# Two pools of tiles change places under the gated stage, and the Gelu's table is loaded at the head of the last block

## The chip, the cores and the metric

One core of one Trainium2 chip runs the whole program. The metric is device time of one execution in microseconds (us). The kernel before was executed three times, and one further execution was profiled.

## What is computed

A decaying linear attention (per token, a state of 64 x 64 per head, here written in chunks), then three bilinear products, then a gated layer. Cut to what matters:

```python
x = attention(q, k, v)                    # 4 x 768 tokens, 8 heads x 64
a, b = x @ w1, x @ w2                     # 512 -> 1024
x = (a * b @ w3) @ w_out                  # 1024 -> 512
h = x @ w_in                              # 512 -> 2048
g = h * (1.0 / (1.0 + np.exp(-1.702 * h)))
return g @ w_out2                         # 2048 -> 512
```

There are 3072 tokens. The weights arrive as 64-bit floats and are rebuilt on the chip.

## The kernel before

Every product of matrices is done three times, on a high part and a low part of each operand (`mm3`, L220 to L223), so that float32 accuracy comes out of a narrower multiplier. High parts are made by a cast, low parts by a subtraction.

The program has four stages, and in each the order of instructions on every engine is the order in which the code issues them (a manual schedule).

- **Attention** (L695 to L761), in 24 chunks, while ScalarE (ACT) and VectorE (DVE) rebuild weights and `w3 @ w_out` is formed.
- **The six blocks** of 512 tokens (L768 to L866). In each, `gate` (L798) makes two products of 12 matmuls and multiplies them, eight times, and `mixed` (L807) adds each into four accumulators. At a block's end the four accumulators are copied out by ACT (L825) and DVE (L823) in turn, into two tiles named `st` under the tag "st" and two under the tag "tmp", and SyncE (SP) stores each to `yd` in DRAM (L826, 256 KB each). The tokens of even blocks lie in one pair of tiles, those of odd blocks in another (`homes["x", 1]`, the pool `p1x`). The last block, number 5, is odd.
- **The gated stage** (`Expand`, L448), four passes over 768 tokens. One pass is eight `quad`s; each makes seven products P1, P5, P6, P2, P3, P7, P4 of six matmuls with 384 columns, and P4 of a quad is issued in the next one (`fourth`), after that one's P5. So the first quad of the stage has 36 matmuls and every later one 42. ACT copies P1, P5, P6 and P7 out of their banks (`copy`, L459) and applies the Gelu (`gated`, L469); DVE adds. A later product of the same bank starts only once ACT has copied the earlier one. Results go to tiles `g`, five buffers, two to a quad, and SP stores them to `gd` (L472, 384 KB each).
- **The last product** (`contract`, L617), from `gd` and `w_out2`.

The weights of the gated stage were split earlier and stored as sixteen blocks `sp` in DRAM. Eight of them, one to a quad, are brought back by eight DMAs of 1792 KB on GpSimd's (POOL's) queue: `run` calls `fetch_left` (L441) for quad n = 0 to 7, which fills the tile `op` of slot SLOT[n]. Those eight slots, and behind them the tiles `g` and the tiles `s` and `u` of `copy`, are laid over memory that the six blocks had used, and the framework puts in the waits that this needs. Per partition a slot takes 14336 bytes, so eight take 114688. Below them lie, from the bottom, the pool `big` (65536 bytes, weights), `p1w` (32768, weights), `p1x` (16384, the odd blocks' tokens) and `p1` (16384: "tmp", then the gate's results "h", then "st"). The first three make 114688 bytes too. So the slots end where `p1` begins, and `g` and `s` lie on `p1`:

```python
SLOT = 0, 1, 5, 6, 7, 2, 3, 4
...
homes = [left_tile(self.pf, x) for x in range(NQ)]
for n in range(NQ):
    fetch_left(n, homes[SLOT[n]])
```

The same table gives the slots that the last product reuses (`OPENING`, L599, and L678); they go by SLOT[n] throughout.

ACT has two loads of its activation table: at L107 at the start (Abs), and at L469, ahead of the first Gelu.

Of the kernel before, what the change touches and what calls it, by code (L numbers as in the profile page):

```python
# [7 lines left out]
F32 = mybir.dt.float32  # L8
F32R = mybir.dt.float32r
I32 = mybir.dt.int32  # L10
AF = mybir.ActivationFunctionType
# [5 lines left out]
P = 128  # L17
# [4 lines left out]
TB = 512  # L22
# [19 lines left out]
def tile_kernel(  # L42
# [13 lines left out]
    nc = tc.nc  # L56
# [1 line left out]
    big = first.enter_context(tc.tile_pool(name="big", bufs=1, reuse_waits="tile"))  # L58
    second, third = (ctx.enter_context(ExitStack()) for _ in range(2))
    edge = ctx.enter_context(tc.tile_pool(name="edge", bufs=1, side="right"))  # L60
    edge.tile([P, 88], F32, name="edge")
    prep = second.enter_context(
        tc.tile_pool(name="prep", bufs=1, side="right", reuse_waits="tile")
    )
# [150 lines left out]
    def weight(i):  # L215
        while complete <= i:
            work(1)
        return parts[i]
# [21 lines left out]
    def halves(key):  # L240
        return [tuple(t[:, d] for t in xhl[key]) for d in range(KD)]
# [191 lines left out]
    left = {}  # L433
    PART = dict(P1=0, P2=1, P4=2, P5=3, P6=4, P7=5, P3=6)

    SLOT = 0, 1, 5, 6, 7, 2, 3, 4

    def left_tile(pool, slot):
        return pool.tile([P, 2, 7, 256], F32R, tag=f"op{slot}", name="op")

    def fetch_left(n, t):  # L441
        left[n] = t
        nc.gpsimd.dma_start(t.rearrange("p a b c -> p a (b c)").bitcast(F32), sp[n])
# [4 lines left out]
    class Expand:  # L448
# [62 lines left out]
        def run(self):  # L511
            self.late, self.open = [], None
# [3 lines that stand above are left out]
            nxt = None  # L516
# [25 lines left out]
    def load_g(n, pool, queue=nc.sync, **at):  # L542
        if n >= len(batches):
            return
        i, b = batches[n]
        raw = raws2[n] = pool.tile([P, 2, 2, TB], F32, name="gr", **at)
        at = 0
        while at < TB:
            s, t0 = divmod(i * TB + at, 2 * TS)
            m = min(TB - at, 2 * TS - t0)  # L550
            for k in range(2):
                queue.dma_start(
                    raw[:, k, :, at : at + m], gd[s][:, 2 * b + k, :, t0 : t0 + m]
                )
            at += m

    def sums(n, pool, **at):
        (b11, b12), (b21, b22) = (
            [raws2[n][:, :, f, h * TU : (h + 1) * TU] for h in range(2)] for f in range(2)
        )  # L560
        t = mid[n] = pool.tile([P, 4, 2, TU], F32, name="gt", **at)
        for x, (a, b) in enumerate(((b12, b11), (b22, t[:, 0]), (b22, b12), (b21, t[:, 1]))):
            nc.vector.tensor_tensor(t[:, x], a, b, ALU.subtract)

    def operand_tiles(n, pool, tags, **at):
        ops[n] = [
            pool.tile([P, 7, 2, TU], F32R, tag=tag, name=f"o{w}", **at)
            for w, tag in zip("hl", tags)
        ]
# [18 lines left out]
    def split_piece(a, b):  # L588
# [3 lines left out]
        else:  # L592
# [7 lines left out]
        (0, 3): lambda p, pf: load_g(0, p, tag="raw"),  # L600
        (1, 3): lambda p, pf: sums(0, pf, tag=f"op{SLOT[0]}"),
        (3, 0): lambda p, pf: (
            operand_tiles(0, pf, [f"op{SLOT[x]}" for x in (1, 2)]),
            split_piece(0, 1),
        ),
        (3, 3): lambda p, pf: split_piece(1, 2),
        (4, 0): lambda p, pf: split_piece(2, 3),
        (4, 1): lambda p, pf: fetch_left(NQ, left_tile(pf, SLOT[3])),
        (4, 3): lambda p, pf: split_piece(3, 5),
        (5, 0): lambda p, pf: split_piece(5, 7),  # L610
        (5, 3): lambda p, pf: load_g(1, pf, tag=f"op{SLOT[0]}"),
        (5, 1): lambda p, pf: fetch_left(NQ + 1, left_tile(pf, SLOT[4])),
        (6, 1): lambda p, pf: fetch_left(NQ + 2, left_tile(pf, SLOT[5])),
# [76 lines left out]
    with tc.manual_schedule():  # L690
        with (
# [62 lines left out]
            while halves_done < 2 * KF:  # L754
                f = halves_done // 2
# [5 lines left out]
            mix_out()  # L761
        with (
            tc.tile_pool(name="p1w", bufs=1, reuse_waits="tile") as p1w,
            tc.tile_pool(name="p1x", bufs=1, reuse_waits="tile") as p1x,
            tc.tile_pool(name="p1", bufs=1, reuse_waits="tile") as p1,
            tc.tile_pool(name="ps1", bufs=1, space=PSUM, reuse_waits="tile") as ps1,
        ):
            homes["wd"], homes["x", 1] = p1w, p1x  # L768

            def reload(key, src, d):  # L770
                x = p1.tile([P, TB], F32, tag="st", bufs=2, name="xr")
                nc.sync.dma_start(x, src[:, d])
                return lambda: split(key, x, d)

            def mm(lhs, xs):
                ps = ps1.tile([P, TB], F32, tag="mm", bufs=4, name="psm")
                for d in range(KD):
                    mm3(ps, lhs[0][:, d], lhs[1][:, d], *xs[d], d == 0, d == KD - 1)
                return ps

            def pair(t):
                hi, lo = (
                    p1.tile([P, TB], F32R, tag="h", bufs=4, name=f"h{x}") for x in "hl"
                )
                nc.scalar.copy(hi, t)  # L785
                nc.vector.tensor_tensor(lo, t, hi.bitcast(F32), ALU.subtract)
                return hi, lo

            def tmp():
                return p1.tile([P, TB], F32, tag="tmp", bufs=2, name="tmp")  # L790


            xs = halves(order[0])
            ahead = None
            todo = []
            acc = None

            def gate(f, xs):  # L798
                w = [x.rearrange("p (m k f) -> p m k f", m=2, k=KD) for x in weight(W12 + f)]
                pa = mm([x[:, 0] for x in w], xs)  # L800
                pb = mm([x[:, 1] for x in w], xs)
                t = tmp()
                nc.scalar.copy(t, pa)
                nc.vector.tensor_tensor(t, t, pb, ALU.mult)  # L804
                return pair(t)

            def mixed(i, f, hl):  # L807
                nonlocal acc
                if f == 0:
                    acc = [  # L810
                        ps1.tile([P, TB], F32, tag=f"acc{e}", name=f"acc{e}")
                        for e in range(KD)
                    ]
                wh, wl = (x[:, f % 2 * DM : (f % 2 + 1) * DM] for x in wmix[f // 2])
                for e in range(KD):
                    r = slice(e * P, (e + 1) * P)
                    mm3(acc[e], wh[:, r], wl[:, r], *hl, f == 0, f == KF - 1)
                if f == KF - 1:
                    for e in range(KD):
                        tag = "st" if e < 2 else "tmp"  # L820
                        t = p1.tile([P, TB], F32, tag=tag, bufs=2, name="st")
                        if e % 2:
                            nc.vector.tensor_copy(t, acc[e])  # L823
                        else:
                            nc.scalar.copy(t, acc[e])  # L825
                        nc.sync.dma_start(yd[i][:, e], t)  # L826

            early = None
            for n, i in enumerate(order):
                last = n == NB - 1  # L830
                nxt = None if last else order[n + 1]
                for f in range(KF):
                    if not last and KF - KD - 2 <= f < KF - 1:
                        ready, ahead = ahead, None
                        if f < KF - 2:
                            ahead = reload(nxt, xd[nxt], f - KF + KD + 2)
                    if n == 0:
                        work_to(min(PAIR_OPS * (W12 + f + 2) + 4, PAIR_OPS * WI + 4))
                    elif not last:
                        work(5)  # L840
                    elif f == 0:
                        while complete < len(tiles):
                            work(1)
                        second.close()
                        py = third.enter_context(
                            tc.tile_pool(name="y", bufs=1, side="right", reuse_waits="tile")
                        )
                        early = operands(0, py)
                        next(early)
                    else:  # L850
                        next(early)
                    hl = gate(f, xs)
                    if todo:
                        late, *args = todo.pop()
                        late(*args)
                    todo.append((mixed, i, f, hl))
                    if not last and KF - KD - 1 <= f < KF - 1:
                        ready()
                    if 0 < n and not last:
                        work(4)  # L860
                    if last and f in (3, 6):
                        next(early)
                if nxt is not None:
                    xs = halves(nxt)
            late, *args = todo.pop()
            late(*args)  # L866
# [97 lines left out]
```

## Time and profile before

| | |
|---|---|
| three executions | 1052.08, 1053.18, 1053.92 us (median 1053.18) |
| the profiled execution | 1055.27 us, of which 1053.5 us is its span |
| PE (TensorE matmuls) busy | 1005.4 us, 95% of the span |
| DVE busy | 666.7 us, 63% |
| ACT busy | 405.5 us, 38% |
| POOL busy | 24.7 us, 2% |
| mean granted TensorE clock | 0.987 of full |

The page gives busy time by engine and the chain that ended last; the trace gives single instructions with their start, their duration and, in brackets, how long the engine had been idle and what ended that. "PEclk" is the granted clock: 1.00 is 2.4 GHz, 0.50 is 1.2 GHz. A DMA has two times, that of its issue (on SP's or POOL's queue) and its landing. q0 is the queue that POOL feeds, q1 that of SP.

### The profile page before, as it was taken

To read this page: it belongs to the slowest core of one execution; us is meant where nothing else is said; L and a number is where in the kernel's file an instruction comes from. 1 tells how busy PE (TensorE), PEld (TensorE's weight loads), DVE (VectorE), ACT (ScalarE), POOL (GpSimd) and SP (SyncE) were. 2 spreads that over 40 slices of the span, in tenths; PEclk is the share of its full clock that TensorE was granted. 3 is DMA by queue.
4 is the path that set the end of the run, shared out by engine and by line. 5 is a ranking of instruction groups with operands and counts; after the bars stand their busy time and mean duration, and the time that the engine had idled before them with its cause. 6 is when DMAs were issued, how large, how long until landed. Compare 5 with 4: busy or idle time off the path is not lost.

```text
span 1053.5 us, 16352 instructions
## 1 busy us (share of the span) xinstructions
PE 1005.4 (95%) x6528; PEld 914.8 (87%) x6528; DVE 666.7 (63%) x1084; ACT 405.5 (38%) x702; POOL 24.7 (2%) x49
## 2 busy tenths in 40 slices
PE   5789999999999999999994999999999999999997
PEld 4678787888888888888884999999999999999997
DVE  4998788856777767733440263453654597787783
ACT  2333334433434444321111555545555344334331
POOL 1110000000000000000000000000001000000000
PEclk9999999999999999999997899999999999999999
DMA  9998765436675766541319423424359943343431
GB/s 348 347 371 282 246 198 185 147 128 219 230 252 207 255 213 224 199 150 40 139 34 426 161 110 135 151 106 165 145 184 407 378 160 121 122 159 120 123 119 40
DMA packets 78012, 204.06 MB, mean 194 GB/s; under 512 B 6512, under 2 KB 28144, under 8 KB 72944
## 3 DMA queue, kind: packets, MB, share of 16 engines
q1 hardware_dynamic: 71744, 147.44, 40.3%
q0 software_dynamic: 6192, 55.58, 13.6%
q8 instruction: 51, 0.84, 0.3%
q14 instruction: 25, 0.20, 0.1%
HBM read 130.64 MB, written 72.35 MB: 193 GB/s over the span
## 4 chain that ended last, share of the span: by engine, by line
PE 84%; DMA 8%; DVE 4%; issue 3%; ACT 1%; POOL 0%; DVEq 0%; POOLq 0%; ACTq 0%
PE psm L223 8%; PE psm L221 8%; PE psm L222 8%; PE m L223 6%; PE m L222 6%; PE m L221 6%; PE acc L221 4%; PE acc L223 4%; PE acc L222 4%; PE a L221 4%; PE a L223 4%; PE a L222 4%; DMA gr<-gd 3%; DMA yd<-st 2%; PE e L221 2%
## 5 line engine op out<-in xcount | busy, mean ns | idle before, releaser
L221 PE MATMUL m<-oh,op 128*128 128x256 f32 x672 | 187.8, 279 | 0.5 <-DVE o L649 0.5
L223 PE MATMUL m<-oh,op 128*128 128x256 f32 x672 | 188.1, 280 | 0.0
L222 PE MATMUL m<-ol,op 128*128 128x256 f32 x672 | 187.7, 279 | 0.0
L223 PE MATMUL psm<-xh,wl 128*128 128x512 f32 x384 | 149.5, 389 | 1.5 <-DVE wl L116 1.5
L222 PE MATMUL psm<-xl,wh 128*128 128x512 f32 x384 | 149.4, 389 | 0.0
L221 PE MATMUL psm<-xh,wh 128*128 128x512 f32 x384 | 149.4, 389 | 0.0
L221 PEld LDWEIGHTS m<-oh,op 128*128 128x128 f32 x672 | 125.9, 187 | 0.8 <-DVE o L649 0.8
L222 PEld LDWEIGHTS m<-ol,op 128*128 128x128 f32 x672 | 126.3, 188 | 0.2 <-DVE ol L586 0.2
L223 PEld LDWEIGHTS m<-oh,op 128*128 128x128 f32 x672 | 126.3, 188 | 0.0
L221 PE MATMUL a<-yh,op 128*128 128x384 f32 x256 | 87.1, 340 | 15.3 <-ACT s L459 11.4
L804 DVE TENSOR_TENSOR tmp<-tmp,psm 128x512 f32<-128x512 f32 x48 | 33.0, 688 | 104.2 <-PE psm L223 93.3
L223 PEld LDWEIGHTS psm<-xh,wl 128*128 128x128 f32 x384 | 72.1, 188 | 17.0 <-DVE wl L116 2.0
L223 PE MATMUL a<-yh,op 128*128 128x384 f32 x256 | 86.7, 339 | 0.0
L222 PE MATMUL a<-yl,op 128*128 128x384 f32 x256 | 86.7, 338 | 0.0
L222 PEld LDWEIGHTS psm<-xl,wh 128*128 128x128 f32 x384 | 72.1, 188 | 15.0
L221 PEld LDWEIGHTS psm<-xh,wh 128*128 128x128 f32 x384 | 72.1, 188 | 14.9
L497 DVE TENSOR_TENSOR s<-c,s 128x384 f32<-128x384 f32 x32 | 17.8, 558 | 98.7 <-PE c L223 98.7
L584 ACT CAST oh<-gr 128x512 fp32r<-128x512 f32 x69 | 38.3, 618 | 102.7 <-PE m L223 59.9
L785 ACT CAST hh<-tmp 128x512 fp32r<-128x512 f32 x48 | 29.8, 621 | 121.7 <-DVE tmp L804 121.7
L221 PE MATMUL acc<-hh,wh 128*128 128x512 f32 x192 | 74.7, 389 | 0.0
L222 PE MATMUL acc<-hl,wh 128*128 128x512 f32 x192 | 74.7, 389 | 0.0
L223 PE MATMUL acc<-hh,wl 128*128 128x512 f32 x192 | 74.7, 389 | 0.0
(99 smaller groups left out, 1889.8 us busy)
## 6 DMA issues: line engine op xcount, KB each, us to landing
op<-sp POOLq DMA_DIRECT2D x16, 1792.0 KB, 11.4
gd<-g SPq DMA_DIRECT2D x64, 384.0 KB, 2.3
qkv<-in_qkv_dram POOLq DMA_DIRECT2D x23, 1024.0 KB, 8.1
raw<-in_w_dram SPq DMA_DIRECT2D x32, 512.0 KB, 5.2
gr<-gd SPq DMA_DIRECT2D x30, 512.0 KB, 4.8
raw<-in_wo_dram SPq DMA_DIRECT2D x24, 512.0 KB, 5.5
raw<-in_wi_dram SPq DMA_DIRECT2D x16, 512.0 KB, 5.0
sp<-wqh SPq DMA_DIRECT2D x16, 512.0 KB, 3.7
```

Source lines behind the costliest of these rows:

```text
L221: nc.tensor.matmul(ps, wh, xh, start=start, stop=False, skip_group_check=True)
L222: nc.tensor.matmul(ps, wh, xl, start=False, stop=False, skip_group_check=True)
L223: nc.tensor.matmul(ps, wl, xh, start=False, stop=stop, skip_group_check=True)
L497: nc.vector.tensor_tensor(s1, c, s1, ALU.add)
L584: nc.scalar.copy(h, x)
L785: nc.scalar.copy(hi, t)
L804: nc.vector.tensor_tensor(t, t, pb, ALU.mult)
```

## The change

Four edits. The pool `p1` is cut in two: `p1h` holds the tiles "h", and `p1` keeps "tmp" and "st". The pools are opened in the order `p1w`, `p1h`, `p1`, `p1x`, so that "h", "tmp" and "st" lie below 114688 bytes, under slot 7, and the odd blocks' tokens lie above, under `g` and `s`. SLOT is changed so that slot 7 is filled last, for quad 7, and slots 2, 3 and 4 for quads 4, 5 and 6. And a tile that was only a spacer is cleared by POOL at the start, and one element of it goes through the Gelu at the head of the last block.

```diff
-    edge.tile([P, 88], F32, name="edge")
+    still = edge.tile([P, 88], F32, name="edge")
+    nc.gpsimd.memset(still, 0.0)
...
-    SLOT = 0, 1, 5, 6, 7, 2, 3, 4
+    SLOT = 0, 1, 5, 6, 2, 3, 4, 7
...
             tc.tile_pool(name="p1w", bufs=1, reuse_waits="tile") as p1w,
+            tc.tile_pool(name="p1h", bufs=1, reuse_waits="tile") as p1h,
+            tc.tile_pool(name="p1", bufs=1, reuse_waits="tile") as p1,
             tc.tile_pool(name="p1x", bufs=1, reuse_waits="tile") as p1x,
-            tc.tile_pool(name="p1", bufs=1, reuse_waits="tile") as p1,
...
-                    p1.tile([P, TB], F32R, tag="h", bufs=4, name=f"h{x}") for x in "hl"
+                    p1h.tile([P, TB], F32R, tag="h", bufs=4, name=f"h{x}") for x in "hl"
...
                         next(early)
+                        nc.scalar.activation(still[:, :1], still[:, :1], AF.Gelu_apprx_sigmoid)
                     else:
```

Three lines are added above most of the program, so its line numbers grow by one to three in the kernel after. The order of the matmuls is the same, and that of DVE and SP too; what differs are ACT and POOL, and what instructions wait for.

**ACT, from the last block's end into the first quad.** Before (DMAHW is an SP transfer that must have landed, DMASW one of POOL's; s and u are the tiles of `copy`):

```order
L825 COPY st<-acc_4400 128x512 [waits PE_49,Activation_49]
L459 COPY s_4779<-a 128x384 [waits DMAHW3_49,DMAHW7_49,DVE_49,PE_49]
L459 COPY s_4787<-e 128x384 [waits PE_49]
L459 COPY u_4795<-a 128x384 [waits PE_49]
L469 ACT_TABLE_LOAD [waits DMAHW1_49,DMAHW0_49]
L469 ACTIVATE g<-s_4779 128x384 [waits DVE_49]
L459 COPY u_4818<-a 128x384 [waits PE_49]
L469 ACTIVATE g<-u_4795 128x384 [waits DVE_49]
L459 COPY s_4834<-a 128x384 [waits PE_49]
L469 ACTIVATE g<-u_4818 128x384 [waits DMAHW6_49,DVE_49]
```

Now:

```order
L827 COPY st<-acc_4405 128x512 [waits PE_49,Activation_49]
L460 COPY s_4785<-a 128x384 [waits PE_49]
L460 COPY s_4793<-e 128x384 [waits PE_49]
L460 COPY u_4801<-a 128x384 [waits PE_49]
L470 ACTIVATE g<-s_4785 128x384 [waits DVE_49]
L460 COPY u_4824<-a 128x384 [waits PE_49]
L470 ACTIVATE g<-u_4801 128x384 [waits DVE_49]
L460 COPY s_4840<-a 128x384 [waits PE_49]
L470 ACTIVATE g<-u_4824 128x384 [waits DVE_49]
```

The waits on the last block's stores (DMAHW7, 1, 0 and 6 are the second, fourth, third and first of its four) are gone, and with them the table load. It stands at the head of the last block, between the cast for the block before and the copy of the block's first gate:

```order
L787 CAST hh<-tmp 128x512 [waits DVE_49]
L852 ACT_TABLE_LOAD
L852 ACTIVATE edge<-edge 128x1
L805 COPY tmp<-psm 128x512 [waits PE_49,Activation_49]
L787 CAST hh<-tmp 128x512 [waits DVE_49]
```

**POOL, the weights of quads 2 to 7** (sp_85 to sp_90 before). Before:

```order
L443 DMA op<-sp_85 128x3584 [waits DMAHW2_49,DMAHW3_49,DMASW5_49,DMAHW5_49,DMASW0_49,DMAHW6_49,DVE_49,PE_49]
L443 DMA op<-sp_86 128x3584 [waits DMAHW2_49,DMAHW1_49,DMAHW3_49,DMASW7_49,DMAHW4_49,DMASW6_49,DVE_49]
L443 DMA op<-sp_87 128x3584 [waits DMAHW6_49,DMAHW7_49,DMAHW5_49,DMAHW0_49]
L443 DMA op<-sp_88 128x3584 [waits DMAHW4_49,DMAHW3_49,DMAHW5_49,DMAHW2_49,PE_49]
L443 DMA op<-sp_89 128x3584 [waits DMAHW4_49,DMAHW5_49,DMAHW3_49,DMAHW2_49]
L443 DMA op<-sp_90 128x3584 [waits DMAHW3_49,DMAHW2_49,DMAHW4_49,DMAHW1_49,Pool_49]
```

Now (sp_86 to sp_91):

```order
L444 DMA op<-sp_86 128x3584 [waits DMAHW2_49,DMAHW3_49,DMASW5_49,DMAHW5_49,DMASW0_49,DMAHW6_49,DVE_49,PE_49]
L444 DMA op<-sp_87 128x3584 [waits DMAHW1_49,DMAHW2_49,DMASW7_49,DMAHW3_49,DMASW6_49,DMAHW4_49,DVE_49,PE_49]
L444 DMA op<-sp_88 128x3584 [waits DMAHW6_49,DMAHW5_49,DMAHW7_49,DMAHW0_49,PE_49]
L444 DMA op<-sp_89 128x3584 [waits DMAHW4_49,DMAHW5_49,DMAHW3_49,DMAHW2_49]
L444 DMA op<-sp_90 128x3584 [waits DMAHW4_49,DMAHW3_49,DMAHW5_49,DMAHW2_49,Pool_49]
L444 DMA op<-sp_91 128x3584 [waits DMAHW3_49,DMAHW4_49,DMAHW2_49,DMAHW5_49,DMAHW1_49,DMAHW6_49,DMAHW0_49,DMAHW7_49,DVE_49,Activation_49]
```

The second now waits for PE too (the matmuls of `mixed` that read the last gate but one's "h", which lies there), the third for the last matmul of the block, and the last for all four stores of the last block. Before, none of the eight waited for those stores.

## Rows read from the trace of the kernel before

**Rows 1.** Waits of PE over the span: us in total, times, longest.

```profile
PE a L221 <- ACT s L459: 11.4, 1, 11.4
PE a L221 <- ACT u L459: 3.9, 2, 3.3
```

**Rows 2.** PE in order of time: start us, us, line, tile; in brackets idle before.

```profile
554.08 0.33 PE L221 MATMUL a<-yh,op 128*128 128x384 f32 x1
...
567.72 0.69 PE L221 MATMUL a<-yh,op 128*128 128x384 f32 x1 [11.37 <-ACT s L459]
...
579.23 0.69 PE L221 MATMUL a<-yh,op 128*128 128x384 f32 x1 [3.33 <-ACT u L459]
...
585.11 0.34 PE L221 MATMUL e<-yh,op 128*128 128x384 f32 x1
...
587.19 0.33 PE L221 MATMUL a<-yh,op 128*128 128x384 f32 x1
...
592.39 0.33 PE L221 MATMUL e<-yh,op 128*128 128x384 f32 x1
```

**Rows 3.** PE by stretch: us, us, busy (instructions), granted clock, DMA share, GB/s.

```profile
567.70:571.40 3.70, 3.68 (x11) 0.50 1.03 433
579.20:585.10 5.90, 5.87 (x18) 0.51 0.37 148
```

**Rows 4.** ACT in order of time, from the last block into quads 0 to 2.

```profile
553.65 0.59 ACT L825 COPY st<-acc 128x512 f32<-128x512 f32 x1 [0.83 <-PE acc L223]
567.19 0.48 ACT L459 COPY s<-a 128x384 f32<-128x384 f32 x1 [12.95 <-DMA yd<-st]
...
576.99 1.28 ACT L469 ACT_TABLE_LOAD   x1 [6.46 <-DMA yd<-st]
...
578.72 0.46 ACT L459 COPY u<-a 128x384 f32<-128x384 f32 x1
...
588.86 0.53 ACT L469 ACTIVATE g<-u 128x384 f32<-128x384 f32 x1
```

**Rows 5.** SP's issues of the last block's four stores, in order of time.

```profile
552.86 2.46 SPq L826 DMA_DIRECT2D yd<-st  x4
```

**Rows 6.** First, second and last of them, each looked at alone: KB, us to landing.

```profile
yd<-st SPq DMA_DIRECT2D x1, 256.0 KB, 9.4
...
yd<-st SPq DMA_DIRECT2D x1, 256.0 KB, 13.5
...
yd<-st SPq DMA_DIRECT2D x1, 256.0 KB, 21.9
```

**Rows 7.** DMA queues in 565 to 570: packets, MB, share of the 16 engines.

```profile
q0 software_dynamic: 147, 1.88, 87.8%
q1 hardware_dynamic: 150, 0.27, 14.2%
```

**Rows 8.** Stores of g issued in 579 to 590: KB, us to landing.

```profile
gd<-g SPq DMA_DIRECT2D x3, 384.0 KB, 2.3
```

**Rows 9.** POOL in order of time, the weights of quads 2 to 7.

```profile
549.10 0.53 POOL L443 DMA_DIRECT2D op<-sp  x1 [31.73 <-PE psm L223]
550.14 1.10 POOL L443 DMA_DIRECT2D op<-sp  x2 [0.51 <-DVE tmp L804]
554.54 1.70 POOL L443 DMA_DIRECT2D op<-sp  x3 [3.29 <-PE acc L223]
```

**Rows 10.** ACT at the last block's head, in order of time.

```profile
489.06 0.59 ACT L803 COPY tmp<-psm 128x512 f32<-128x512 f32 x1 [4.08 <-PE psm L223]
```

**Rows 11.** ACT's copies of 128x512 by line: busy us, mean ns.

```profile
L825 ACT COPY st<-acc 128x512 f32<-128x512 f32 x12 | 7.0, 585 | 3.8 <-PE acc L223 3.8
...
L651 ACT COPY o<-m 128x512 f32<-128x512 f32 x6 | 3.5, 585 | 20.6 <-PE m L223 20.6
```

**Rows 12.** POOL at the start, in order of time.

```profile
0.24 0.10 POOL L947 MEMSET const-float32-0.0<- 128x1 f32 x1 [0.24 <-issue]
...
3.47 1.00 POOL L708 MEMSET state<- 128x512 f32 x2
```

## The prediction

> **What bounds the kernel now.** First the waits of PE, since PE is busy for 95% of the span: whatever shortens this kernel has to fill a gap in PE or raise its clock. The longest single wait of all, 11.4 us, ends with ACT's first copy of the gated stage, and another of 3.3 us ends with a copy of ACT just behind it [rows 1]. Then PE in order of time, for the place: the stage's first matmul starts at 554.08, the third product stands until 567.72, and the second quad's first continuation until 579.23 [rows 2]. Then ACT in the same stretch, for the reason: ACT was free from 554.24 on, and its copy of P1 began at 567.19 because a store of the last block had to land; the table load then stood until 576.99 for another one, and everything on ACT is in order behind it [rows 4]. Last the clock: behind each of the two gaps PE runs 11 and 18 matmuls at 0.50 and 0.51 of its clock [rows 3], so a gap costs twice.
>
> What is waited for is not work but memory: the copy of P1 writes where the second store still reads, the first Gelu where the third and the fourth do. The four stores are issued from 552.86 to 555.3 [rows 5] and take 9.4, 13.5 and, the last one, 21.9 us [rows 6], though a larger store takes 2.3 us once the queues are quiet [rows 8]. Between lies POOL's queue: six weight loads of 1792 KB each go out from 549.10 to 556.2 [rows 9], and while they run SP's queue moves 0.27 MB in 5 us where POOL's moves 1.88 MB, with as many packets on each [rows 7]. That is 54 GB/s against 376.
>
> **The pools and the slots: what goes.** The new order lists no store of the last block for any ACT instruction of the first quads; the first one left is the Gelu of quad 2's second tile, which waits for the first store of the gated stage itself. So ACT's copy of P1 should follow its product as it does later in the stage. Size of the gain, by counting matmuls: from 554.08 to the first P3 matmul of quad 1 at 585.11 [rows 2] lie 36 + 30 = 66 matmuls. A full quad of 42 takes 592.39 - 585.11 = 7.28 us [rows 2], 0.1733 us each, so 66 take 11.44 us. They took 31.03. **Gain 19.6 us**: the two gaps of 11.4 and 3.3 us [rows 1], and about 4.5 us of slow clock (3.70 + 5.90 us for 29 matmuls that take 5.03 at full pace [rows 3]), rest rounding. I take the whole of it, since the first quad has shorter distances than later ones only at one point (P6 follows P5 directly, without a P4 between), and there P1's copy has 1.04 us of P5 to hide in and takes 0.48 [rows 4]. The bounds of this term are 13.9 (below, the second case) and 19.6.
>
> **What is late next: the weights.** Quads 0 and 1 have theirs early, as before. Quad 2's are asked for at 549.10, unchanged. Quad 3's wait for about ten matmuls more of the last block, some 1.5 us, and quad 4's move from the second issue to the third, from 550.7 to 554.54 [rows 9]. POOL's queue has loads waiting all the same, so it runs through from 550: five loads are 9.2 MB, at 376 GB/s [rows 7] 24.4 us, until about 575. That order is also the order of need: quad 2 starts at 567.6, quad 6 at 596.7 and quad 7 at 554.08 + (36 + 252) x 0.1733 = 604.0. Quad 7's now wait for all four stores. These land at the latest as before, at 576.9 [rows 5, 6]; then 1792 KB need 4.9 us at 376 GB/s. Ready by 584, twenty us ahead. Nothing else is queued behind that load on POOL until the fourth pass. **Cost 0.**
>
> **What is late next: the five buffers of g.** The stage's first stores are now issued from about 561 on, into a queue that still holds the last block's four. The trace of before has no store of g beside weight loads, so this is the cost to bound. The Gelu of quad 2's second tile needs the first store landed. It would come 1.67 us into quad 3 (588.86 against 587.19 [rows 2, 4]), and quad 3 starts at 554.08 + 120 x 0.1733 = 574.9; so it is due at 576.5. PE would notice only if the copy of P5 behind it (0.48) missed P3, 30 matmuls into the quad: the Gelu (0.53) may start as late as 574.9 + 5.2 - 1.0 = 579.1. By the rows: the stores on SP's queue landed one after the other, 4.9 us apart at 54 GB/s [rows 6, 7]; the fourth lands about 575 to 577, when POOL's five loads are through, and the first store of g goes next, alone, in about 1 us (2.3 from issue to landing [rows 8]). It lands at 577 to 578: ACT late by a us, PE not at all. Cost 0, bound below. The Trainium skill (DMA: Bandwidth & Descriptors, on queues, rings and completion order) speaks against counting on that: each engine takes the queues with work in turn, packet by packet, and completion on one issuing engine's queue is not promised in order. By that rule the store would be slowed for as long as POOL's last load is in flight; the equal packet counts of rows 7 agree with the turn-taking, the even spacing of rows 6 shows order kept here. By the rows the sum is 19.4, by the rule 13.7 to 16.5, which is my second case.
>
> **The table load.** It moves into a gap of 4.08 us in which ACT stands before the last block's first gate [rows 10]. 1.28 us [rows 4], plus an activation on one element, for which the nearest row, of 384 columns, is 0.53 as an upper end and 0 the lower: 1.8 at most, hidden by 2.3. At its old place the 1.28 us were on the path; they are in the 19.6 already. ACT's copies run under the Gelu's table for the rest of the block: the same copy takes 585 ns under either table [rows 11]. **Cost 0.** Without its cover it would cost up to 1.8.
>
> **The clearing of the spacer.** One memset of 128x88 stands on POOL ahead of the first load of attention's operands. Between 0.10 for one column and 0.50 for 512 [rows 12], by columns about **0.2 us**; the attention stage starts with that load, so I put it on the path. Bounds 0 and 0.5.
>
> **Sum.** 19.6 - 0.2 = 19.4 us. The profiled execution took 1055.27, so 1035.9 there; the median of the runs is 1053.18, 2.09 lower: **1033.8 us**. Less than 0.2% (2.1 us) either way could not be told from no change.
>
> **The rivals.**
> - *The new wait on g* (chance 0.10). If the last weight load starts before the first store of g is through, that store gets some 70 GB/s (its rows are 3 KB, those of `yd` 2 KB, against rows 7's 54) and 393 KB take 5.6 us: landing at 582 instead of 579.1. PE loses 2.9 us, and the same again if its clock falls as after the 3.3 us gap (5.90 us for 18 matmuls instead of 3.12 [rows 3]). Time 1036.7 to 1039.5. For it: equal packets on both queues [rows 7]. Against it: POOL may issue that load only when the last block's stores have landed, and the store of g then stands at the head of SP's queue already. (It is the case that the page of the Trainium skill named above would have.)
> - *Only the table load counts* (0.03). Should a wait on the stores remain that the order does not name, only the 1.28 us on the chain go [rows 4]: 1051.9, within 0.2%. Against it: the order of ACT and the sizes of the pools.
> - *Quad 7 starves* (0.03). Its weights wait for the stores and are asked for last. PE stands at 604.0 if they have not landed, each us costs one, and above 3 us the slow clock adds some 2.8. Slower than before from a landing at about 604 + 16.6 = 620.6 on, 44 us after the last store; landing at 623 gives 1055.6. Against it: 4.9 us of transfer, with nothing on POOL's queue ahead of it.
> - The order shows the waits gone, so that the change does nothing at all has no chance of its own beside the second of these.
>
> **How the numbers follow.** My forecast has 0.84, its own range 1032 to 1036 (the runs shown lie within 1.1 us of their median, the memset within 0.3, ACT's hiding within 1). The range reaches up to the new wait on g: 1031.8 to 1039.5, which leaves out the last two rivals. Faster by over 0.2%: 0.84 + 0.10 = 0.94; within 0.2%: 0.03; slower: 0.03.
>
> **What would show it.** In the profile after: PE without a gap from the last block into the gated stage, the clock at 1.00 from block to block; the four stores as slow as before, and nobody waiting for them but POOL; one table load near 485; the chain without "DMA yd<-st". Quad 3 shows whether ACT waits for a store of g, and whether PE notices. The forecast is wrong if PE stands in quads 3 to 7, or if anything of ACT's in the first quad still ends its wait on a DMA.

## The result and the profile after

Four executions of the kernel after took 1033.55 to 1034.55 us, median **1034.1 us**; four of the kernel before had a median of 1053.52. The ratio is 0.9818, with a 95% interval of 0.9801 to 0.9835, so the change is faster by 19.4 us, and outside the 0.2% that could not be told from no change. The forecast was 1033.8.

The profiled execution of after took 1034.44 us, of which 1032.6 are its span. PE was busy for 999.0 us, 97% of it. The waits of PE over the whole span of the kernel after (us in total, times, longest):

```profile
PE s L283 <- DMA qkv<-in_qkv_dram: 14.5, 5, 7.3
PE s L283 <- DVE pt L295: 5.0, 5, 1.8
PE u L309 <- ACT state L323: 1.8, 2, 1.5
PE psm L224 <- DVE wl L117: 1.5, 1, 1.5
PE m L223 <- DVE ol L587: 1.4, 1, 1.4
...
PE a L222 <- ACT u L460: 0.6, 1, 0.6
```

The row of 11.4 us is gone and that of 3.9 us has shrunk to 0.6 [rows 1]; what leads the list now, as it did before with 15.0, are attention's operands at the start. PE in order of time in the gated stage of after, the same places as in [rows 2]:

```profile
552.21 0.33 PE L222 MATMUL a<-yh,op 128*128 128x384 f32 x1
...
563.68 0.33 PE L222 MATMUL e<-yh,op 128*128 128x384 f32 x1
...
570.96 0.33 PE L222 MATMUL e<-yh,op 128*128 128x384 f32 x1
```

From the stage's first matmul to quad 1's first P3 there are now 563.68 - 552.21 = 11.47 us, where there were 31.03: 19.56 us less. This stretch of 66 matmuls is called the **measure** below, since it is the same in every kernel. PE by stretch in after (us, us, busy, granted clock, DMA share, GB/s) shows no gap, and the clock at 1.00 through the places of [rows 3]:

```profile
552.20:563.70 11.50, 11.50 (x68) 1.00 1.01 425
556.20:585.00 28.80, 28.80 (x169) 1.00 1.02 413
```

ACT of after in order of time: the table load and its companion, then the copy of P1, the first Gelu, and the Gelu of quad 2's second tile.

```profile
483.12 1.28 ACT L852 ACT_TABLE_LOAD   x1
484.41 0.20 ACT L852 ACTIVATE edge<-edge 128x1 f32<-128x1 f32 x1
487.18 0.59 ACT L805 COPY tmp<-psm 128x512 f32<-128x512 f32 x1 [2.57 <-PE psm L224]
...
553.47 0.48 ACT L460 COPY s<-a 128x384 f32<-128x384 f32 x1 [1.10 <-PE a L224]
...
557.26 0.53 ACT L470 ACTIVATE g<-s 128x384 f32<-128x384 f32 x1 [1.22 <-DVE s L498]
...
576.16 0.53 ACT L470 ACTIVATE g<-u 128x384 f32<-128x384 f32 x1 [1.35 <-DMA gd<-g]
```

From the gated stage on no wait of ACT ends on `yd` any more [rows 4]. (Within the six blocks five waits of ACT ahead of `tmp` still do, 10.5 us in all against 11.1 before; PE stands for none of them.) The table load and its companion ended with 2.57 us of the gap to spare. One wait on a store is new, 1.35 us in quad 3, and no wait of PE answers to it.

The stores themselves are no faster. Second and last of the last block's four in after (KB, us to landing), and the two queues in 565 to 570, where q0 is POOL's and q1 SP's:

```profile
yd<-st SPq DMA_DIRECT2D x1, 256.0 KB, 13.3
...
yd<-st SPq DMA_DIRECT2D x1, 256.0 KB, 22.1
```

```profile
q0 software_dynamic: 144, 1.84, 85.8%
q1 hardware_dynamic: 147, 0.27, 13.9%
```

13.3 and 22.1 stood at 13.5 and 21.9 [rows 6], and 144 against 147 packets stood at 147 against 150 [rows 7]. Only POOL waits for them now, with quad 7's weights (POOL of after in order of time). The trace names a store of `gd` as the releaser of the last row; by the waits listed with the change the DMA waits for the four of `yd`, the last of which landed at about 575.

```profile
547.23 0.53 POOL L444 DMA_DIRECT2D op<-sp  x1 [31.73 <-PE psm L224]
549.72 0.53 POOL L444 DMA_DIRECT2D op<-sp  x1 [1.96 <-PE acc L223]
552.67 1.70 POOL L444 DMA_DIRECT2D op<-sp  x3 [2.42 <-PE acc L224]
575.96 0.53 POOL L444 DMA_DIRECT2D op<-sp  x1 [21.58 <-DMA gd<-g]
```

The spans differ by 20.9 us, more than the measure's 19.56. The gated stage starts 1.87 us earlier in after, which is not the change: in 76 to 80 us, in attention, the clock was 0.57 in the profiled execution of before and 1.00 in that of after, which is about 0.43 x 4 = 1.7 us. Of the ten kernels told of below it was 0.57 to 0.73 in seven and 1.00 in three, of which one has none of the change's edits. From quad 2's first P3 to the end after took 0.53 us more (461.64 against 461.11). 19.56 + 1.87 - 0.53 = 20.9.

### The profile page after: what moved, and what is told of

Same layout as the page of the kernel before. It is cut to its first block, busy times and chain, and to the rows that moved or that the text cites. A ratio compares the mean times of both kernels' runs of the same rounds, so it can differ in the third digit from the quotient of the medians.

```text
span 1032.6 us, 16346 instructions
## 1 busy us (share of the span) xinstructions
PE 999.0 (97%) x6528; PEld 909.4 (88%) x6528; DVE 666.7 (65%) x1084; ACT 406.2 (39%) x703; POOL 24.9 (2%) x50
## 4 chain that ended last, share of the span: by engine, by line
PE 88%; DVE 4%; DMA 4%; issue 2%; ACT 1%; POOL 0%; DVEq 0%; SPq 0%; POOLq 0%
PE psm L224 8%; PE psm L223 8%; PE psm L222 8%; PE m L222 7%; PE m L224 7%; PE m L223 7%; PE a L223 4%; PE a L222 4%; PE a L224 4%; PE acc L223 4%; PE acc L222 4%; PE acc L224 4%; PE e L223 2%; PE e L222 2%; PE e L224 2%
## 5 line engine op out<-in xcount | busy, mean ns | idle before, releaser
L222 PE MATMUL a<-yh,op 128*128 128x384 f32 x256 | 85.6, 334 | 0.6 <-ACT u L460 0.6
L224 PE MATMUL a<-yh,op 128*128 128x384 f32 x256 | 85.5, 334 | 0.0
## 6 DMA issues: line engine op xcount, KB each, us to landing
op<-sp POOLq DMA_DIRECT2D x16, 1792.0 KB, 10.9
```

What stands on the lines that cost most here:

```text
L222: nc.tensor.matmul(ps, wh, xh, start=start, stop=False, skip_group_check=True)
L224: nc.tensor.matmul(ps, wl, xh, start=False, stop=stop, skip_group_check=True)
```

## The experiments

**The theory.** ACT wrote into memory that the last block's slow stores were reading. The new order of the pools alone takes that away; slots and table load bring no time. **Rivals:** the table load has a share of its own; the slots make the stores faster or save the weights; the edits bring their gain only together. Times are medians with the kernel before run beside; the measure comes from the profiled execution of each.

| kernel | us | before | ratio, 95% | measure, us |
|---|---|---|---|---|
| after | 1034.10 | 1053.52 | 0.9801 to 0.9835 | 11.47 |
| pools alone | 1035.06 | 1053.23 | 0.9809 to 0.9841 | 11.46 |
| pools and slots, no table edit | 1034.56 | 1054.02 | 0.9768 to 0.9830 | 11.46 |
| pools and table, old slots | 1034.75 | 1054.02 | 0.9761 to 0.9836 | 11.47 |
| table alone | 1050.64 | 1054.02 | 0.9937 to 0.9981 | 28.57 |
| slots alone | 1053.07 | 1054.02 | 0.9958 to 0.9997 | 29.47 |
| before, loads cut in two | 1045.38 | 1053.18 | 0.9904 to 0.9948 | 20.66 |
| after, 4 buffers of g | 1037.27 | 1053.18 | 0.9820 to 0.9895 | 11.46 |
| after, 6 buffers of g | 1035.20 | 1053.18 | 0.9771 to 0.9874 | 11.47 |
| old slots, 4 buffers of g | 1037.33 | 1053.40 | 0.9823 to 0.9864 | 11.47 |
| after, 3 buffers of g | 1046.83 | 1053.40 | 0.9923 to 0.9963 | 11.47 |

Single executions of some of these, and of the kernel before, came out some 7 us shorter than their median (1027.0 with a median of 1034.75); where two profiled ones gained it is told at the end. The measure does not contain it.

**1. The pools alone.** The kernel before with this:

```diff
+            tc.tile_pool(name="p1h", bufs=1, reuse_waits="tile") as p1h,
             tc.tile_pool(name="p1", bufs=1, reuse_waits="tile") as p1,
+            tc.tile_pool(name="p1x", bufs=1, reuse_waits="tile") as p1x,
...
-                    p1.tile([P, TB], F32R, tag="h", bufs=4, name=f"h{x}") for x in "hl"
+                    p1h.tile([P, TB], F32R, tag="h", bufs=4, name=f"h{x}") for x in "hl"
```

> The kernel before with the new order of the pools alone: slots, spacer and table load as before. Theory (the memory that the copies and the Gelu write is the whole cause): first matmul of the gated stage to quad 1's first P3 in 11.47 us, 1034 us, within 1.5 of the changed kernel; the stores land by about 565 as in old_slots. Rival (the edits only bring their gain together): a wait of PE on ACT in the first two quads, 1 us or more, 1036 us and up.

The measure is 11.46 and the time 1035.06, with no wait of PE on ACT in the first quads. The stores landed sooner here than in before, in 9.7 to 10.1 us, but that is not why ACT ran: its first copy began at 555.74, some 7 us before the first of them had landed. The theory holds: within the noise of the times, the new order of the pools is the whole gain.

**2. Without the table edit.** The kernel after, and:

```diff
-    still = edge.tile([P, 88], F32, name="edge")
-    nc.gpsimd.memset(still, 0.0)
+    edge.tile([P, 88], F32, name="edge")
...
-                        nc.scalar.activation(still[:, :1], still[:, :1], AF.Gelu_apprx_sigmoid)
```

> The tiles change places and the slots are the new ones; the Gelu on one element and the clearing of the spacer are left out, so the table is loaded again behind the copy of P1 in the first gated quad. Theory (the whole gain is the waits on the stores): the copy of P1 ends about 556.0, the Gelu behind it is due at 557.3, and the load's 1.28 us fit between them almost whole. PE waits for nothing new: 1034.1 us, within 0.5 of the changed kernel. Rival (the early table load has a share of its own): the load stands on the path once more, 1.3 us or more: 1035.4 to 1036.8 us.

1034.56 us and a measure of 11.46: the rival falls, by the measure, since the time alone lies less than 1 us from the rival's range. ACT of this kernel in order of time (its stage starts 1.15 us later than in after):

```profile
556.70 0.48 ACT L459 COPY u<-a 128x384 f32<-128x384 f32 x1 [0.56 <-PE a L223]
557.20 1.28 ACT L469 ACT_TABLE_LOAD   x1
558.49 0.53 ACT L469 ACTIVATE g<-s 128x384 f32<-128x384 f32 x1
559.82 0.48 ACT L459 COPY u<-a 128x384 f32<-128x384 f32 x1 [0.80 <-PE a L223]
```

The load begins when the copy ends, and the Gelu follows at 558.49, where after's, shifted by 1.15, stands at 558.41. ACT has 1.22 us of idle time ahead of its first Gelu in after, and the load of 1.28 fits into it but for 0.08. The Trainium skill (ScalarE: Activation LUTs, What ACT_TABLE_LOAD costs) gives 1283 ns for the load and 1380 ns more for a drain. The 1.28 us agree; of the drain nothing is seen, 0.02 us lie between copy and load and 1.29 between the load's start and the Gelu's.

**3. The table alone.** The kernel before with the edit that the last one left out, so that ACT still waits for the stores.

> The kernel before with the Gelu on one element in its last block and the clearing, and nothing else: ACT still waits for the last block's stores. Theory: the 11.4 us wait stays; the second gap goes from 3.3 to about 2.0 us since the load no longer follows the store's landing. 1.3 us gained at least, up to 4.1 if the shorter gap leaves the clock at full: 1049.4 to 1052.2 us. Rival (the table alone makes the change): 1034 us. Second rival (the table is hidden anyway): 1053.5 us.

1050.64 us, measure 28.57, so 2.46 us less than before. The first theory holds, between its two numbers: PE's second gap fell from 3.33 to 2.11, by 1.22, the first by 0.12, and the rest is a shorter stretch at half clock behind it (12 matmuls, below; 18 in [rows 3]). The table load is worth something only where a late store stands ahead of it.

**4. The old slots.** The kernel after with `SLOT = 0, 1, 5, 6, 7, 2, 3, 4`.

> The changed kernel with the table of slots of before, so that quad 4's weights go where the last block's stores read, and the loads of quads 5 to 7 stand behind that one on POOL. Theory: from about 553 on only the loads of quads 2 and 3 run beside the stores, which then land by 562 to 566; POOL goes on there, and quads 4 to 7 have their weights at about 571, 576, 581 and 586, ahead of 582, 589, 597 and 604. 1034 us, within 1: the slots bring no time. Rival (quad 4's load waits until about 575, when the last store lands in the changed kernel): weights at 580, 585, 590 and 595, still ahead, but by 2 us; a store later than that makes PE stand in quad 4: 1036 to 1042 us.

1034.75 us, measure 11.47. POOL of this kernel, and the landings of two `yd` stores that its trace shows together (KB, median us):

```profile
549.18 0.53 POOL L444 DMA_DIRECT2D op<-sp  x1 [31.73 <-PE psm L224]
551.68 0.53 POOL L444 DMA_DIRECT2D op<-sp  x1 [1.96 <-PE acc L223]
565.45 2.08 POOL L444 DMA_DIRECT2D op<-sp  x4 [13.25 <-DMA gd<-g]
```

```profile
yd<-st SPq DMA_DIRECT2D x2, 256.0 KB, 9.9
```

With four loads held back behind the stores, the stores landed in 9.7 to 9.9 us instead of up to 22.1, and POOL went on at 565.45. The first of the four landed 7.6 us after its issue, at 573, and quad 4 began at 554.16 + 162 x 0.1733 = 582.2; the last two, looked at together, took 19.9 us, to about 587, and quads 6 and 7 began at 596.8 and 604.1. PE waited for none. So the old slots would have done, and by the time they give there is nothing in the new ones. They spare ACT the wait of 1.35 us in quad 3, but give it a longer one: the tokens of the next pass (`yr`) are loaded beside the four weight loads, DVE waits for them, and ACT waits for DVE, as DVE and ACT of this kernel show. In after DVE does not wait for `yr`. PE stands for neither.

```profile
593.87 0.96 DVE L410 TENSOR_TENSOR yt<-yr 128x768 f32<-128x768 f32 x1 [3.05 <-DMA yr<-yd]
...
597.78 0.53 ACT L470 ACTIVATE g<-s 128x384 f32<-128x384 f32 x1 [3.34 <-DVE s L498]
```

**5. The slots alone.** The kernel before with `SLOT = 0, 1, 5, 6, 2, 3, 4, 7`.

> The kernel before with the new table of slots alone: ACT waits for the last block's stores as before, and one load fewer is asked for before they are issued. Theory: POOL's queue has loads waiting through the whole of the stores' time all the same, so the stores get the same 54 GB/s and PE waits as long: 1053.5 us, within 1. Rival (what counts is how many bytes were asked for ahead of the stores): the second store lands about 4.9 us earlier and the wait of 11.4 us is cut to 6.5: 1047 to 1049 us.

1053.07 us, within 1 us of before, so the rival is out: PE's first gap is 10.9 us and not 6.5, and the last store still took 21.4 us. The measure is 1.56 shorter, by a first gap of 10.89 instead of 11.37, a second of 2.60 instead of 3.33, and a third or so of a us of slow clock; that this comes of the one load fewer asked for ahead of the stores is argued, not shown.

**6. Why the stores are slow.** The kernel before, and each load of weights of quads 0 to 7 as two DMAs:

```diff
-        nc.gpsimd.dma_start(t.rearrange("p a b c -> p a (b c)").bitcast(F32), sp[n])
+        for w in range(2) if n < NQ else ():
+            nc.gpsimd.dma_start(t[:, w].rearrange("p b c -> p (b c)").bitcast(F32), sp[n][:, w])
+        if n >= NQ:
+            nc.gpsimd.dma_start(t.rearrange("p a b c -> p a (b c)").bitcast(F32), sp[n])
```

> The kernel before with each of the gated stage's eight loads of weights cut into two, so that a row in them has 7168 bytes instead of 14336; the same bytes on the same queue, in twice as many packets. Theory (the two queues take turns packet by packet, so a queue's share goes by the size of its packets): the stores' rows of 2048 bytes get 2048 of every 9216 bytes of 430 GB/s, about 95 GB/s instead of 54; a store of 256 KB takes 2.75 us, the second lands at about 562, the last at about 567; the 11.4 us wait falls to about 5, the other goes: 1040 to 1045 us. Rival (the stores wait for the bytes that were asked for before them): no change, 1053.5 us.

The queues of this kernel in 557 to 560, the four stores each looked at alone, and ACT's two waits:

```profile
q0 software_dynamic: 154, 0.98, 78.0%
q1 hardware_dynamic: 154, 0.28, 24.4%
```

```profile
yd<-st SPq DMA_DIRECT2D x1, 256.0 KB, 6.9
...
yd<-st SPq DMA_DIRECT2D x1, 256.0 KB, 13.2
```

```profile
561.92 0.48 ACT L462 COPY s<-a 128x384 f32<-128x384 f32 x1 [8.50 <-DMA yd<-st]
567.51 1.28 ACT L472 ACT_TABLE_LOAD   x1 [2.25 <-DMA yd<-st]
```

Equal packets again, and the bytes now stand as 0.98 to 0.28, 3.5 to 1, as the rows of 7168 and 2048 bytes do; before, it was 1.88 to 0.27, 7 to 1, as 14336 to 2048 [rows 7]. 0.28 MB in 3 us are 93 GB/s, against the 95 expected; the second store had landed by 561.9 and the last by 567.5, where 562 and 567 were expected. The kernel with the old slots adds a third pair of rows, stores of `g` with 3072 bytes beside the whole loads; its queues in 584 to 587:

```profile
q0 software_dynamic: 77, 1.10, 85.8%
q1 hardware_dynamic: 77, 0.24, 19.4%
```

That is 4.6 to 1, where 14336 to 3072 is 4.7 to 1. So, in these three cases, **the queues take turns by the row, and the size of the other queue's row sets the price of a store**. The Trainium skill (DMA: Bandwidth & Descriptors, Queues, rings and completion order) has each engine taking the queues with work in turn, packet by packet, and these runs agree. The measure fell by 10.4 us and the time by 7.8, to 0.4 above the range expected; the rest was given back past the stage. PE waits 1.94 us for DVE's `ol` there (0.5 at most at DVE's `o` in before), and the clock falls to 0.72 in 820 to 825; both rows are shown in the last section.

**7. Buffers of g.** The kernel after with 4, 6 and 3 buffers, and the old slots with 4:

```diff
-            g = [self.p.tile([P, 2, TS], F32, tag="g", bufs=5, name="g") for _ in range(2)]
+            g = [self.p.tile([P, 2, TS], F32, tag="g", bufs=4, name="g") for _ in range(2)]
```

> The changed kernel with four buffers of g instead of five. Theory: the first Gelu that needs the memory of a stored g is now one of quad 2's first tile, due at 571.8; the first store of the gated stage lands at 576.2, so ACT is 4.3 us late and PE stands for 2 to 3 us, and perhaps at half clock behind it: 1036 to 1040 us. Rival (ACT's distance to PE takes this too): as the changed kernel, 1034.1 us.

1037.27 us, as the theory had it. ACT was 5.69 us late at one Gelu, PE stood 2.00 us, and quad 3 took 2.30 us more than its 7.28. PE of this kernel, the matmul behind the gap and the windows around it:

```profile
579.78 0.44 PE L222 MATMUL a<-yh,op 128*128 128x384 f32 x1 [2.00 <-ACT u L460]
```

```profile
577.00:580.00 3.00, 1.00 (x6) 1.00 1.03 414
580.00:583.00 3.00, 3.00 (x18) 1.00 1.00 326
```

> The changed kernel with six buffers of g. Theory: ACT's wait of 1.35 us for the store of g goes, and since PE did not stand for it the time stays: 1034.1 us, within 0.5. Rival (PE did notice it): 1 us or more faster, 1033 us or less.

1035.20 us, with an interval that holds after's ratio. The time alone does not settle it: it is 1.1 us above after's, more than the 0.5 expected, and the four executions lie 9 us apart. But ACT's wait for a store of `g` is gone from the trace, and PE's measure and quad 3 are as in after: that wait cost nothing. By the trace the theory holds.

> Four buffers of g, as in g4, but with the table of slots of before. Theory (the store of g is late in g4 because POOL's loads and the last block's slow stores stand ahead of it): with the old slots POOL stops asking after quad 3's load, the last block's stores land about 565, and so the first store of g, issued about 561, lands by 567, ahead of the Gelu that needs its memory (due 573.8 in that run's time): ACT does not wait, PE does not stand, 1034 to 1035 us. Rival (four buffers are too few by themselves): as g4, 2.3 us lost in quad 3, 1037 us.

Half right. At the place of g4's wait ACT stands no more, and PE runs through quad 3: the store of `g` was late there because of what stood ahead of it. But the four loads that POOL issues at 565.64 then meet the later stores of `g`. ACT waits 2.41 us until 589.99, which PE does not notice, and 3.59 us until 595.33, behind which PE stands 0.95 in quad 5; 1.24 us are lost there. ACT and PE of this kernel, and the store of `g` issued at 579.23 (KB, us to landing):

```profile
595.33 0.52 ACT L470 ACTIVATE g<-u 128x384 f32<-128x384 f32 x1 [3.59 <-DVE yt L410]
...
596.27 0.45 PE L222 MATMUL e<-yh,op 128*128 128x384 f32 x1 [0.95 <-ACT s L460]
```

```profile
gd<-g SPq DMA_DIRECT2D x1, 384.0 KB, 16.0
```

The trace names DVE's `yt` as what ended the 3.59 us. But DVE had made this Gelu's input by 591.47, and with the old slots and five buffers the same Gelu ran at 591.22, ahead of the same `yt`. The store landed at 579.2 + 16.0 = 595.2, so it is taken to be the cause. The median of 1037.33 is above what this gives; the profiled execution, 1036.93, also reached the gated stage 2.36 us later than after's.

> The changed kernel with three buffers of g. The Gelu of quad 1's second tile, due at 567.4, now needs the first store of g, which lands at about 576.2: ACT 8.8 us late. The prediction allowed such a Gelu 2.6 us before PE notices, so PE stands about 6.2 us. Theory (a gap costs twice, as in the prediction's rivals): 11 to 18 matmuls behind it run at half clock, 1.9 to 2.8 us more: 1042 to 1043 us. Rival (behind a long busy stretch the clock stays at 1.00, as it did behind g4's gap of 2.0 us): 1040 to 1041 us.

ACT came 8.73 us late and PE stood 6.08, as worked out (8.8 and 6.2). Behind it, PE of this kernel by stretch:

```profile
571.80:577.90 6.10, 0.02 (x1) 0.75 0.91 345
577.90:581.70 3.80, 3.80 (x12) 0.50 1.07 342
```

Twelve matmuls at 0.50: 8.1 us are lost there, 6.25 up to the end of the gap and 1.86 behind it, as the theory gave (6.2 and 1.9 to 2.8). The rival is out here. The time is nearly 4 us above the 1042 to 1043 expected, for a cause that the expectation did not have: a second gap of 3.90 us at 797.01, at the end of the fourth pass, with eleven matmuls at 0.50 behind it. ACT had stood 5.51 us there, again for a store of `g`.

## Why the prediction was right

- **The gain, 19.6 us.** The measure fell by 19.56. The working by counting matmuls gave 11.44 us for the new stretch, and 11.47 was measured. The new order of the pools alone gives it, so its cause (memory that the stores still read) is shown, not argued.
- **The stores stay slow, and nobody minds.** 22.1 us for the last, as forecast; nobody but POOL waits for them.
- **The weights, cost 0.** Quad 7's load went out at 575.96, when the prediction had the last store landing at the latest at 576.9, and PE had no wait for weights. One size in it was wrong: the load took 11.6 us from issue to landing and not 4.9. POOL's queue moved nothing until 580.5, while SP's moved the next pass's tokens and stores of `g`, which the working had left out; why the load started so late is not shown. It landed at 587.6, and quad 7 began at 552.21 + 288 x 0.1733 = 602.1, so there were 14.5 us to spare, where the working had twenty. This part was more cautious than it had to be: the old slots, with four loads held back, cost nothing either.
- **The five buffers of g, cost 0.** This was the closest call, and it came out to a few tenths: the prediction had the store landing at 577 to 578, ACT late by a us, the last moment at 579.1. After starts its stage 1.87 us earlier, and its Gelu ran at 576.16, which is 578.0 on before's scale, 1.35 us late. The distance of 2.6 us that it allowed ACT is what two kernels show: 8.73 late, 6.08 stood with three buffers, and 3.59 late, 0.95 stood with the old slots and four. (At the Gelu of a quad's first tile, with four buffers, it was 5.69 late and 2.00 stood.) The rival, in which PE loses 2.9 us at this Gelu, did not come. Whether a load of POOL's would have slowed the store, as that rival has it, after does not test: the last one went out at 575.96, when the store had all but landed.
- **The table load, cost 0.** Hidden at its new place by 2.57 us more than it needed. What the prediction did not say is that it would have been hidden at its old place too, once the stores no longer stood ahead of it: "they are in the 19.6 already" is right for the sum, and experiment 2 shows that this share needed no edit.
- **The clearing, 0.2 us: mis-sized.** The memset took 0.17 us but fell into a wait that POOL had anyway; the first load of attention stood at 1.25 us before and stands at 1.28. 0.03 us, inside the bounds given. Of POOL at the start of after, in order of time:

```profile
0.73 0.17 POOL L62 MEMSET edge<- 128x88 f32 x1 [0.29 <-POOLq L950]
1.28 2.23 POOL L266 DMA_DIRECT2D qkv<-in_qkv_dram  x4 [0.37 <-issue]
```

The sum of 19.4 was met by the medians, 1053.52 - 1034.10 = 19.4. That they meet it to the tenth is luck: single executions of before lay 1.8 us apart, the 0.2 of the memset was 0.03, and 0.53 us were lost behind quad 2. In the profiled executions it was 20.8, by the clock in attention.

## What to carry to other kernels

Memory that is being stored is free only when the store has landed, here 9 to 22 us after its issue. So memory that is stored last before a stage belongs under what that stage fills last, and not under the first thing its busiest chain writes. Where a small store lags behind a bulk load, compare packets and bytes of the two queues: equal packets with unequal bytes say that cutting the load's rows, or holding back loads that are not yet needed, speeds the store (here from 21.9 us to 13.2 and to 9.7). And a gap is to be priced with the half clock that may stand behind it, and a wait with the distance that it must first use up.

## What the runs showed that was not expected

**A gap does not always cost twice.** Behind a gap of 2.00 us, which followed a long stretch of full work, the clock stayed at 1.00 in the kernel with four buffers. Behind one of 2.11 us in the kernel with the table edit alone, some 10 us after the gap of 11.25 us, it fell to 0.54 (PE of that kernel by stretch):

```profile
577.30:581.00 3.70, 3.63 (x12) 0.54 0.75 314
```

Behind 3.90 and 6.08 us, both after full work, it fell to 0.50. Full work ahead of a gap does not spare the clock by itself: in the kernel with the halved loads a gap of 1.94 us in the last product, behind 17 us of full work, brought it to 0.50 to 0.59 for 3.7 us. PE of that kernel, the matmul behind the gap and the windows around it:

```profile
819.26 0.48 PE L222 MATMUL m<-ol,op 128*128 128x256 f32 x1 [1.94 <-DVE ol L589]
```

```profile
810.00:815.00 5.00, 5.00 (x45) 1.00 1.03 433
820.00:825.00 5.00, 5.00 (x33) 0.72 1.06 431
```

The kernel with the pools alone shows the same behind a gap of 1.91 us at 811.16. So neither the length of a gap nor full work ahead of it decides alone; what does, these runs do not settle.

**The last product has two paces at the same granted clock.** Its matmuls of 256 columns start 0.118 us apart in after and in most profiled executions, and 0.113 in those of the kernels with six buffers and with the table alone. PE of the kernel with six buffers, then of after:

```profile
880.00:900.00 20.00, 20.00 (x179) 1.00 0.39 120
```

```profile
880.00:900.00 20.00, 20.00 (x173) 1.00 0.32 107
```

From 800 us to the end PE was busy 217.33 us against 224.09, 6.8 us, about what the short executions are shorter by. In both profiled executions that have the quicker pace it begins, early in the stage, behind two distances of 0.22 us in a row, with no wait (838.2 with six buffers, 855.5 with the table alone); the kernel with the slots alone shows the same two at 856.5 and stays at the slower pace. A single execution of the kernel before was as short (1045.89, with a median of 1053.18), so this is not the change's doing. What decides it stays open.
